# The opening of an attention-and-MoE kernel: a third load through SyncE, casts on ScalarE and GpSimd, and a new list of steps

## The chip, the cores and the metric

One core of a Trainium2 chip. The metric is the device time of one execution in microseconds; of several executions the median is taken. TensorE (PE) multiplies, VectorE (DVE), ScalarE (ACT) and GpSimd (POOL) work on its operands and results, SyncE (SP) issues transfers. POOL issues transfers too. Each engine works through its own list in order.

## What is computed

```python
# q, k, v: (8, 8, 576, 64) f32; w_in: (512, 2048); w_out: (2048, 512)
scores = q @ k.transpose(0, 1, 3, 2) / sqrt(64)
scores = where((rel >= 0) & (rel < 64), scores, -1e9)   # rel = row - column
attn = softmax(scores) @ v                              # windowed, causal
x = attn.transpose(0, 2, 1, 3).reshape(4608, 512)
h = x @ w_in
out = (h * cos(h)) @ w_out
```

## The kernel before

The 4608 tokens are worked through in nine tiles of 512 rows. For each tile PE forms h from x and w_in, ACT takes a sine of h (shifted by half of pi), DVE multiplies the two into a gate, and PE multiplies that by w_out. The attention of the next batch is woven into this by a planner that gives each piece a due time. That holds from the second tile on. Up to the end of the first tile the order is written out by hand: the string FIRST (line 45) is split into steps, and the loop at line 661 runs them one after the other. Each step appends its instructions to the lists of the engines that it uses. An engine therefore meets its instructions in the order of the string, and a wait at the head of its list holds up all that stands behind.

A step has a letter code, then numbers, then at times an engine (a is ACT, d is DVE, p is POOL, s a transfer by SP). Heads go in pairs 0 to 3. A digit that follows a score step is a PSUM bank of five.

- Lq0.p and Lk0.p load q and k of batch 0, pair p; Lq1 and Lk1 those of batch 1. Pair 0 of batch 0 is loaded as f32 by SP into a tile called rows (load_plain, line 154) and cast to bf16 by the step cq or ck (cast_plain, line 159). All the others are loaded by POOL with the cast in the transfer (load_heads, line 147). Lv, Lwi and Lwo load v, and w_in and w_out in quarters, all through POOL.
- tq, tk (batch 0) and Tq, Tk (batch 1) transpose a pair on PE, in 18 products of 64 by 64 (line 202). pq, pk, Pq, Pk copy the result from PSUM to SBUF. Their PSUM tiles come from a pool of three.
- s.p.g (line 295) forms the scores of a group of four blocks of 64 rows: two products that lay the mask into the bank (line 306), then eight of q with k (line 313). Group 0 of a pair is the first half of the tile's rows, group 1 the second. m is the maximum on DVE (line 323), e four exponentials on ACT (line 340), i the reciprocal of the sums on DVE (line 350), n the product of both (line 357, on POOL or DVE), w the transposition of the weights on PE (line 373), c its copy.
- z and y copy halves of v to the other half of the partitions. v.a.g multiplies the weights by v for half of the heads, x.a.g copies that to xT. When x.0.0 and x.1.0 are there, h for the first 256 rows can begin.
- h.g.f (line 424) forms two blocks of h for half g of the rows, S its sine (ACT), g its gate (DVE). tb and tb2 load ACT's tables for the sine and for the exponential. o.q.m (line 443) is a quarter of the second product for 128 rows, four matmuls; oc copies it out.
- Gs, Gm, Ge, Gi, Gn, Gw, Gc, Gp are the same parts of the attention for groups 8 to 18: the last block of batch 0 (8), and batch 1 (9 to 18, of three or four blocks each). Here Gm adds the mask itself (line 328), a block at a time. Gw transposes on PE; Gc lets SP transpose by a transfer. V and X close the next tile's x.

A transfer of POOL's waits until the one eight places ahead of it in POOL's list has landed.

Of the kernel before, what the change touches and what calls it, by code (L numbers as in the profile page):

```python
# [10 lines left out]
def _safe_warn(msg, *a, **kw):  # L11
# [3 lines left out]
F32 = mybir.dt.float32  # L15
# [14 lines left out]
RC = 9  # L30
# [5 lines left out]
DIRECT = (0, 7, 8)  # L36
OUTS = 3
FILL = (6, 12)
TURNED = {4: 2, 5: 2, 6: 2, 7: 6}
FAST = (7, 8)  # L40
PRODUCTS = ("P1", "P2", "P6", "P5", "P7", "P3", "P4")
# [1 line left out]


FIRST = (
# [18 lines left out]
)  # L64


# [1 line left out]
def kernel(  # L68
# [9 lines left out]
    nc = tc.nc  # L78
    B, H, S, D = q.shape
    assert (B, H, S, D) == (8, 8, 576, 64)  # L80
    scale = 1.0 / math.sqrt(D)
    d_model = H * D
    d_ff = moe_w_in.shape[1]
    n_ff = d_ff // 128
    MT = 512
# [6 lines left out]
    att = ctx.enter_context(tc.tile_pool(name="att", bufs=3))  # L92
    moe = ctx.enter_context(tc.tile_pool(name="moe", bufs=2))
# [16 lines left out]
    st = {}  # L110
# [11 lines left out]
    def copy(engine, out, in_):  # L122
        {"a": nc.scalar.copy, "p": nc.gpsimd.tensor_copy}.get(engine, nc.vector.tensor_copy)(out, in_)  # L123
# [20 lines left out]
    def rows_tile(name):  # L144
        return ld.tile([128, NC * H * D], BF16, tag=name, name=name)

    def load_heads(name, b, p0=0, n=PAIRS):
        if (name, b) not in st:
            st[name, b] = rows_tile(name)[:, 0:PAIRS * RC * D].rearrange("p (a x) -> p a x", a=PAIRS)
        src = {"q": q, "k": k}[name][b, 2 * p0:2 * p0 + 2 * n]  # L150
        nc.gpsimd.dma_start(out=st[name, b][:, p0:p0 + n],
                            in_=src.rearrange("(a h) (p c) d -> (h p) a (c d)", h=2, c=RC))

    def load_plain(name):
        rows = moe.tile([128, 2, d_model], F32, tag="out", name="rows", bufs=OUTS).rearrange("p a f -> p (a f)")[:, 0:RC * D]
        st["rows", name] = rows
        nc.sync.dma_start(out=rows, in_={"q": q, "k": k}[name][0, 0:2].rearrange("h (p c) d -> (h p) (c d)", c=RC))

    def cast_plain(name, engine):
        if (name, 0) not in st:  # L160
            st[name, 0] = rows_tile(name)[:, 0:PAIRS * RC * D].rearrange("p (a x) -> p a x", a=PAIRS)
        copy(engine, st[name, 0][:, 0], st.pop(("rows", name)))

    def load_chunk(name, b, c):
        if (name, b) not in st:
# [29 lines left out]
    def transposed(name, b, p):  # L195
# [7 lines left out]
        else:  # L203
            for c in range(TURNED.get(b, 0) if name == "q" else 0, NC):
                nc.tensor.transpose(t_ps[:, NP * c:NP * c + NP], of[:, c, 128 * p:128 * p + 128], ident[:NP, :NP])  # L205
# [9 lines left out]
    def put_q(b, p, engine=None):  # L215
        if b > 1:
            lo = TURNED.get(b, 0) * NP
            copy(engine, qsets[b % 2][:, p, lo:], st.pop(("tq", b, p))[:, lo:])
# [38 lines left out]
    for b in range(2, B):  # L257
        alone = NU // 2 if b == 3 else NU - 1
        steps = [(0, 2), (2, 4)], [(alone,)] + [(5, 7), (7, 9)] if b == 3 else [(4, 6), (6, 8), (alone,)]
# [35 lines left out]
    def g_scores(n, which):  # L295
        s_ps = bank(BANKS[which], "s_ps")
        units = groups[n]
        if n == FILL[1]:
            nc.tensor.matmul(out=s_ps, lhsT=ident, rhs=mask16[:, 0:4].rearrange("p u c -> p (u c)"), start=True, stop=True,
# [66 lines left out]
    def g_trans(n):  # L366
        w, u = st.pop(("w", n)), len(groups[n])
        if n in direct:
            st["tw", n] = t_ps = ps_t.tile([128, GF, 128], BF16, tag="t", name="tw_ps")
            for i in range(GF if n == FILL[0] else 0):  # L370
                nc.tensor.transpose(t_ps[:, i], ident, ident)
# [189 lines left out]
    def at(time, fn, *args):  # L561
        plan.append((time, len(plan), fn, args))
# [26 lines left out]
    for b in range(2, B):  # L589
        t0 = T * (b - 1)  # L590
        for c in range(TURNED.get(b, 0)):
            at(t0 - T + (24.3 if b == 4 else 23.4 if c < 2 else 26.4) + 0.01 * c, turn_q, b, c)
        for p in range(PAIRS if TURNED.get(b) != NC else 0):
            t_q = t0 + (2 if b == 2 else 1) + (3.3 if b == 2 else 3.5) * p
# [8 lines left out]
        for c in range(5):  # L603
            at(t0 + (8 if TURNED.get(b) == NC else 0.5) + c, load_v, b, c)
        for half_ in range(2):
# [16 lines left out]
    for n in range(16):  # L622
        i, f = divmod(n, 4)
# [12 lines left out]
    def spread_first(lo, hi):  # L636
        return lambda i, engine: spread_v(0, i, engine, lo, hi)

    steps = {"Lq0": lambda p: load_heads("q", 0, p, 1) if p else load_plain("q"),
             "Lk0": lambda p: load_heads("k", 0, p, 1) if p else load_plain("k"),  # L640
             "cq": lambda engine: cast_plain("q", engine), "ck": lambda engine: cast_plain("k", engine),
             "Lq1": lambda p: load_heads("q", 1, p, 1), "Lk1": lambda p: load_heads("k", 1, p, 1),
             "Lv0": lambda c: load_v(0, c), "Lv1": lambda c: load_v(1, c), "Lq2": lambda c: load_chunk("q", 2, c), "Lk2": lambda c: load_chunk("k", 2, c),
             "Lwi": lambda i: load_w_in(i * d_ff // W_PARTS, (i + 1) * d_ff // W_PARTS),
# [22 lines left out]
    for mt in range(1, n_mt):  # L667
# [5 lines left out]
        for ff in range(n_ff):  # L673
# [8 lines left out]
            e = ff % 2  # L682
# [54 lines left out]
```

## Time and profile before

| | us |
|---|---|
| median of 3 runs | 304.21 (302.83 to 304.63) |
| the profiled execution, its own time | 303.25 |
| its span, from first to last instruction | 301.5 |
| PE busy in the span | 291.7 (97%) |
| DVE, ACT, POOL busy | 233.9, 232.1, 209.1 |

The profiled execution lies 0.96 us under the median, and 1.8 us of its time lie around the span. PE's busy time is counted from modelled ends of overlapping matmuls; where it matters, the distance from one start to the next is the better measure. Idle time of an engine other than PE costs nothing by itself.

### The profile page before, as it was taken

To read this page: it belongs to the slowest core of one execution; us is meant where nothing else is said; L and a number is where in the kernel's file an instruction comes from. 1 tells how busy PE (TensorE), PEld (TensorE's weight loads), DVE (VectorE), ACT (ScalarE), POOL (GpSimd) and SP (SyncE) were. 2 spreads that over 40 slices of the span, in tenths; PEclk is the share of its full clock that TensorE was granted. 3 is DMA by queue.
4 is the path that set the end of the run, shared out by engine and by line. 5 is a ranking of instruction groups with operands and counts; after the bars stand their busy time and mean duration, and the time that the engine had idled before them with its cause. 6 is when DMAs were issued, how large, how long until landed. Compare 5 with 4: busy or idle time off the path is not lost.

```text
span 301.5 us, 8520 instructions
## 1 busy us (share of the span) xinstructions
PE 291.7 (97%) x2936; PEld 163.8 (54%) x2936; DVE 233.9 (78%) x915; ACT 232.1 (77%) x781; POOL 209.1 (69%) x238
## 2 busy tenths in 40 slices
PE   3989999999999999999999999999999999999996
PEld 2768854644455445444454445445544454785485
DVE  3798887898887886788678865887588658985794
ACT  5899699877987699769986998699978997304610
POOL 8899568996999689986998799878995860000000
PEclk9999999999999999999999999999999999999999
DMA  7999999999999994999999999999699944003013
GB/s 144 176 205 194 197 188 143 96 139 175 222 116 99 234 143 94 100 149 199 181 106 150 186 159 121 128 196 176 120 97 133 203 88 157 0 3 141 1 35 107
DMA packets 158732, 41.47 MB, mean 138 GB/s; under 512 B 146976, under 2 KB 154336, under 8 KB 158688
## 3 DMA queue, kind: packets, MB, share of 16 engines
q0 software_dynamic: 100192, 18.06, 84.0%
q1 hardware_dynamic: 58352, 22.79, 40.8%
q8 instruction: 23, 0.38, 0.5%
q14 instruction: 21, 0.17, 0.2%
q10 hardware_dynamic: 144, 0.07, 0.1%
HBM read 36.70 MB, written 9.44 MB: 153 GB/s over the span
## 4 chain that ended last, share of the span: by engine, by line
PE 80%; DMA 10%; ACT 6%; POOL 1%; issue 1%; DVE 0%; POOLq 0%; SPq 0%
PE h_ps L460 37%; PE out_ps L697 23%; PE out_ps L547 8%; DMA w_out<-in_moe_w_out_dram 6%; ACT e L340 5%; PE out_ps L443 3%; PE o_ps L392 3%; PE s_ps L291 2%; DMA wT<-w 2%; DMA k<-in_k_dram 2%; PE tq_ps L205 1%; PE s_ps L313 1%; POOL w L357 1%; PE s_ps L306 0%; ACT kT L123 0%
## 5 line engine op out<-in xcount | busy, mean ns | idle before, releaser
L460 PE MATMUL h_ps<-xT,w_in 128*128 128x512 bf16 x512 | 115.1, 379 | 0.2
L686 DVE TENSOR_TENSOR gT<-h_ps,sin 128x512 bf16<-128x512 f32 x128 | 85.2, 688 | 25.8 <-ACT sin L683 25.2
L683 ACT ACTIVATE sin<-h_ps 128x512 f32<-128x512 f32 x128 | 73.8, 598 | 37.3 <-PE h_ps L460 37.0
L340 ACT ACTIVATE e<-s,negm 128x128 f32<-128x128 f32 (+1 forms) x256 | 97.1, 381 | 2.0 <-DVE negm L328 1.0
L697 PE MATMUL out_ps<-w_out,gT 128*128 128x512 bf16 x384 | 85.3, 379 | 0.0
L357 POOL TENSOR_TENSOR w<-e,rden 128x512 bf16<-128x512 f32 (+1 forms) x68 | 69.1, 1034 | 17.0 <-DVE rden L350 12.6
L460 PEld LDWEIGHTS <-w_in 128*128 128x128 bf16 x512 | 48.9, 98 | 54.4
L697 PEld LDWEIGHTS <-gT 128*128 128x128 bf16 x384 | 36.5, 98 | 43.1
L328 DVE CUSTOM_DVE_ANT_0 s<-s_ps,mask 128x128 f32<-128x128 f32 (+1 forms) x256 | 56.0, 277 | 2.0 <-PE s_ps L313 1.7
L340 ACT ACTIVATION_READ_ACCUMULATOR e<-s,negm 128x1 f32 x256 | 48.0, 188 | 0.0
L168 POOL DMA_DIRECT2D q<-in_q_dram x36 | 28.6, 794 | 13.5 <-DMA v<-in_v_dram 5.3
L174 POOL DMA_DIRECT2D v<-in_v_dram x40 | 34.2, 869 | 1.1 <-DMA q<-in_q_dram 1.1
L168 POOL DMA_DIRECT2D k<-in_k_dram x36 | 28.5, 792 | 1.3 <-DVE gT L686 0.6
L350 DVE RECIPROCAL rden<-den 128x4 f32<-128x4 f32 (+1 forms) x73 | 12.2, 167 | 18.8 <-ACT e L340 18.5
L123 POOL COPY v<-v 64x1536 bf16<-64x1536 bf16 (+3 forms) x16 | 22.9, 1433 | 0.4
L328 DVE DVE_READ_ACCUMULATOR2_ANT negm<- 128x1 f32 x256 | 21.3, 83 | 0.0
L123 DVE CAST xT<-o_ps 128x512 bf16<-128x512 f32 x24 | 15.6, 680 | 4.9 <-PE o_ps L392 4.7
L443 PE MATMUL out_ps<-w_out,gT 128*128 128x512 bf16 x64 | 14.8, 379 | 0.2 <-DMA w_out<-in_moe_w_out_dram 0.2
L424 PE MATMUL h_ps<-xT,w_in 128*128 128x256 bf16 x128 | 14.7, 273 | 0.0
L547 PEld LDWEIGHTS <-sums 128*128 128x128 bf16 x136 | 12.2, 98 | 2.0 <-DVE sums L492 0.4
L424 PEld LDWEIGHTS <-w_in 128*128 128x128 bf16 x128 | 12.3, 98 | 1.4
L123 ACT CAST xT<-o_ps 128x512 bf16<-128x512 f32 x12 | 7.1, 612 | 6.4 <-PE o_ps L392 6.4
(85 smaller groups left out, 312.4 us busy)
## 6 DMA issues: line engine op xcount, KB each, us to landing
out_dram<-out_sb SPq DMA_DIRECT2D x16, 512.0 KB, 7.7
v<-in_v_dram POOLq DMA_DIRECT2D x32, 128.0 KB, 6.0
q<-in_q_dram POOLq DMA_DIRECT2D x36, 96.0 KB, 8.6
k<-in_k_dram POOLq DMA_DIRECT2D x36, 96.0 KB, 9.0
w_in<-in_moe_w_in_dram POOLq DMA_DIRECT2D x4, 512.0 KB, 9.0
w_out<-in_moe_w_out_dram POOLq DMA_DIRECT2D x4, 512.0 KB, 11.3
q<-in_q_dram POOLq DMA_DIRECT2D x7, 144.0 KB, 6.3
k<-in_k_dram POOLq DMA_DIRECT2D x7, 144.0 KB, 6.2
```

The costliest lines, as they stand in the source:

```text
L123: {"a": nc.scalar.copy, "p": nc.gpsimd.tensor_copy}.get(engine, nc.vector.tensor_copy)(out, in_)
L168: nc.gpsimd.dma_start(out=st[name, b][:, c].rearrange("p (h d) -> p h d", h=H), in_=src.rearrange("h p d -> p h d"))
L174: nc.gpsimd.dma_start(out=vt.rearrange("p (h d) -> p h d", h=H), in_=v[b, :, c * 128:c * 128 + n, :].rearrange("h p d -> p h d"))
L328: nc.vector.tensor_tensor_reduce(out=s[:, u, c], in0=s_ps[:, u, c], in1=mask[:, 2 - j % 2 if j else 0, c], scale=-scale if b else -1.0, sc ...
L340: nc.scalar.activation(e[:, u, c], s[:, u, c], AF.Exp, bias=negm[:, u:u + 1], scale=1.0 if n < n_first else -1.0, accum_out=den[:, u:u + 1])
L357: (nc.gpsimd if engine == "p" else nc.vector).tensor_tensor(out=w[:, 0:u], in0=e[:, 0:u], op=ALU.mult, in1=rden[:, 0:u].unsqueeze(2).to_br ...
L424: nc.tensor.matmul(out=h_ps[:, half * e:half * e + half], lhsT=w_in_sb[:, ks, ff * 128:ff * 128 + 128], rhs=st["xT", 0][:, ks, half * g:ha ...
L460: nc.tensor.matmul(out=st["h", ff], lhsT=w_in_sb[:, ks, ff * 128:ff * 128 + 128], rhs=st["xT", mt][:, ks], start=start, stop=stop)
L547: nc.tensor.matmul(out=to[n_] if split else to[:, e], lhsT=lhs[name][f // 2][:, f % 2, 128 * e:128 * e + 128], rhs=rhs[name][:, f, lo:hi], ...
L683: nc.scalar.activation(sin, h_ps, AF.Sin, bias=math.pi / 2.0)
L686: nc.vector.tensor_tensor(out=gt[:, e], in0=h_ps, in1=sin, op=ALU.mult)
L697: nc.tensor.matmul(out=o_ps[e], lhsT=gT[ff // 2][:, ff % 2, ms * 128:ms * 128 + 128], rhs=w_out_sb[:, ff], start=ff == 0, stop=ff == n_ff - 1)
```

## The change

A table PLAIN says how many pairs of batch 0 are loaded as f32 by SP: two of q, one of k. So Lq0.1 moves from POOL's queue to SP's, and cast_plain gets the pair as an argument. In the new list ACT casts both pairs of q (cq.0.a, cq.1.a) and POOL the pair of k (ck.0.p); before, DVE cast q and ACT cast k. The string FIRST is new from the first step to the last. It holds the same steps, with these differences: one load more by SP, one cast more, and the three copies of v that SP made by transfers (zB.0.s, zB.1.s, zC.s) are done by DVE and POOL. The engines of many copies differ too.

```diff
+PLAIN = {"q": 2, "k": 1}
...
-    "io Lq0.0 Lk0.0 mk cq.d mc ck.a tq.0 Lq0.1 pq.0.d Lk0.1 tk.0 pk.0.a s.0.0.0 Lq0.2 tq.1 tk.1 m.0.0 pq.1.a s.0.1.1 "
-    "Lk0.2 tq.2 pk.1.d s.1.0.2 Lq0.3 Lk0.3 tk.2 s.1.1.3 e.0.0 tq.3 m.0.1 Lq1.0 Lk1.0 Lq1.1 pq.2.d pk.2.d Lk1.1 tk.3 "
...
+    "Lq0.0 io Lk0.0 mk Lk0.1 Lq0.1 mc cq.0.a Lq0.2 Lk0.2 Lk0.3 tq.0 ck.0.p tk.1 tk.0 cq.1.a pq.0.d pk.0.d s.0.0.4 "
+    "tq.1 s.0.1.1 pk.1.a pq.1.a Lq0.3 Lk1.1 tq.2 m.0.0 s.1.0.2 tk.2 e.0.0 tk.3 m.0.1 pq.2.d pk.2.d m.1.0 i.0.0 "
+    "pk.3.a tq.3 Lk1.0 Lv0.1 Lq1.1 Lq1.0 pq.3.d Lwi.0 Lv0.0 e.0.1 s.2.0.0 Tk.1 e.1.0 s.1.1.1 s.3.0.4 s.2.1.2 "
...
-    def load_plain(name):
-        rows = moe.tile([128, 2, d_model], F32, tag="out", name="rows", bufs=OUTS).rearrange("p a f -> p (a f)")[:, 0:RC * D]
...
+    def load_plain(name, p):
+        if (name, p) == ("k", 1):
+            rows = att.tile([128, 2, MT], F32, tag="xT", name="rows", bufs=2).rearrange("p a f -> p (a f)")[:, 0:RC * D]
+        else:
+            rows = moe.tile([128, 2, d_model], F32, tag="out", name="rows", bufs=OUTS).rearrange("p a f -> p (a f)")[:, 0:RC * D]
...
+    def load_first(name, p):
+        if p < PLAIN[name]:
+            load_plain(name, p)
+        else:
+            load_heads(name, 0, p, 1)
...
+    steps = {"Lq0": lambda p: load_first("q", p), "Lk0": lambda p: load_first("k", p),
+             "cq": lambda p, engine: cast_plain("q", p, engine), "ck": lambda p, engine: cast_plain("k", p, engine),
```

Three places show what the lists of the engines became. The first is ACT, from the masks' casts to the second half of the exponentials: the cast of k or q, copies of transposed pairs (kT, qT0) out of PSUM, and groups of four exponentials (e). Before:

```order
L141 CAST mask16_83<-mask_82 128x128
L123 CAST k_108<-rows_96 128x576
L123 COPY kT_151<-tk_ps_132 128x576
L224 ACTIVATE qT0_75<-tq_ps_165 128x576
L340 ACTIVATE e_281,den_282<-s_ps_153,negm_203 128x128 x4
L340 ACTIVATE e_373,den_374<-s_ps_206,negm_306 128x128 x4
L224 ACTIVATE qT0_75<-tq_ps_287 128x576
L340 ACTIVATE e_382,den_383<-s_ps_238,negm_335 128x128 x4
```

And with the change:

```order
L143 CAST mask16_83<-mask_82 128x128
L125 CAST q_110<-rows_92 128x576
L125 CAST q_110<-rows_105 128x576
L125 COPY kT_175<-tk_ps_135 128x576
L230 ACTIVATE qT0_75<-tq_ps_188 128x576
L346 ACTIVATE e_274,den_275<-s_ps_177,negm_242 128x128 x4
L125 COPY kT_175<-tk_ps_280 128x576
L346 ACTIVATE e_335,den_336<-s_ps_207,negm_299 128x128 x4
```

The copy of a fourth pair now stands ahead of the second group of exponentials instead of behind it, and it is a copy of k; the two casts of q stand ahead of all.

The second place is POOL, from its first load to its first products of exponentials and reciprocals (w). Before:

```order
L151 DMA q<-in_q_dram 128x576
L151 DMA k<-in_k_dram 128x576
...
L174 DMA v_77<-in_v_dram 128x8x64 x4
L190 DMA w_in<-in_moe_w_in_dram 128x4x512 x3
L357 TENSOR_TENSOR w<-e,rden 128x512 x7
L190 DMA w_in<-in_moe_w_in_dram 128x4x512
```

With the change, where the first row is pair 1 of k (Lk0.1) and the CAST is ck.0.p:

```order
L153 DMA k<-in_k_dram 128x576
L153 DMA q<-in_q_dram 128x576
L153 DMA k<-in_k_dram 128x576 x2
L125 CAST k<-rows 128x576
...
L196 DMA w_in<-in_moe_w_in_dram 128x4x512
L180 DMA v_77<-in_v_dram 128x8x64 x2
L363 TENSOR_TENSOR w<-e,rden 128x512
L125 COPY v_77<-v_77 64x512
L196 DMA w_in<-in_moe_w_in_dram 128x4x512
L180 DMA v_77<-in_v_dram 128x8x64
L363 TENSOR_TENSOR w<-e,rden 128x512 x2
L196 DMA w_in<-in_moe_w_in_dram 128x4x512
```

The second and the third quarter of w_in moved behind products that wait for exponentials, and pair 1 of k is now the first load of this queue. On PE the transposition of that pair (tk_ps_135, the step tk.1) follows directly on tq.0 and stands ahead of tk.0 and of the first scores; before, the order was tq.0, tk.0, the first scores, tq.1, tk.1.

The third place is DVE around the last gates (gT), where the attention of batch 1 begins. Before, there stand the reciprocal of group 10 (rden_1092), the maximum of group 14 (s_1095), the last gate (gT_932) and the reciprocal of group 9 (rden_1108):

```order
L123 COPY kT_455<-tk_ps_1047 128x576
L350 RECIPROCAL rden_1092<-den_983 128x3
L328 ISA s_1095,negm_1094<-s_ps_1066,mask_82 128x128
...
L436 TENSOR_TENSOR gT_932<-h_ps_941,sin_955 128x2x256
L348 MEMSET e_1026 128x64
L350 RECIPROCAL rden_1108<-den_1027 128x4
```

With the change, the reciprocals of groups 11 and 12 (rden_1084, rden_1092) and the maxima of groups 13 and 14 (s_1087, s_1110):

```order
L442 TENSOR_TENSOR gT_942<-h_ps_964,sin_996 128x2x256
L354 MEMSET e_1044 128x64
L356 RECIPROCAL rden_1084<-den_1045 128x4
L334 ISA s_1087,negm_1086<-s_ps_1072,mask_82 128x64
...
L356 RECIPROCAL rden_1092<-den_1059 128x3
L334 ISA s_1110,negm_1109<-s_ps_1094,mask_82 128x128
...
L363 TENSOR_TENSOR w_1125<-e_1058,rden_1092 128x384
```

The maximum of group 14 (s_1110) now stands behind the reciprocal of group 12, which needs the tenth exponential after the table's load; on PE the scores of group 15 (Gs.15.3) need the bank that this maximum reads.

More of the change, by code (lines that the diff above doesn't have):

```diff
@@ L152, in load_heads, with cast_plain @@
                             in_=src.rearrange("(a h) (p c) d -> (h p) a (c d)", h=2, c=RC))
-    def load_plain(name):
-        rows = moe.tile([128, 2, d_model], F32, tag="out", name="rows", bufs=OUTS).rearrange("p a f -> p (a f)")[:, 0:RC * D]
-        st["rows", name] = rows
-        nc.sync.dma_start(out=rows, in_={"q": q, "k": k}[name][0, 0:2].rearrange("h (p c) d -> (h p) (c d)", c=RC))
-    def cast_plain(name, engine):
+    def load_plain(name, p):
[3 more added lines that the diff above has]
+            rows = moe.tile([128, 2, d_model], F32, tag="out", name="rows", bufs=OUTS).rearrange("p a f -> p (a f)")[:, 0:RC * D]
+        st["rows", name, p] = rows
+        src = {"q": q, "k": k}[name][0, 2 * p:2 * p + 2]
+        nc.sync.dma_start(out=rows, in_=src.rearrange("h (p c) d -> (h p) (c d)", c=RC))
+    def cast_plain(name, p, engine):
         if (name, 0) not in st:
             st[name, 0] = rows_tile(name)[:, 0:PAIRS * RC * D].rearrange("p (a x) -> p a x", a=PAIRS)
-        copy(engine, st[name, 0][:, 0], st.pop(("rows", name)))
+        copy(engine, st[name, 0][:, p], st.pop(("rows", name, p)))
     def load_chunk(name, b, c):
@@ L637, in spread_first @@
         return lambda i, engine: spread_v(0, i, engine, lo, hi)
-    steps = {"Lq0": lambda p: load_heads("q", 0, p, 1) if p else load_plain("q"),
-             "Lk0": lambda p: load_heads("k", 0, p, 1) if p else load_plain("k"),
-             "cq": lambda engine: cast_plain("q", engine), "ck": lambda engine: cast_plain("k", engine),
+    def load_first(name, p):
[5 more added lines that the diff above has]
+             "cq": lambda p, engine: cast_plain("q", p, engine), "ck": lambda p, engine: cast_plain("k", p, engine),
              "Lq1": lambda p: load_heads("q", 1, p, 1), "Lk1": lambda p: load_heads("k", 1, p, 1),
```

32 rows, old and new, of the table FIRST are left out of this document.

## Prediction

> **What bounds the kernel now.** I read the busy times of four stretches first, then the list in order of time of PE, then the chain that ended last, then ACT, DVE and the transfers. The four stretches (duration, then busy time of PE, of its weight loads, of DVE, ACT and POOL):
>
> ```profile
> 0.00:21.90 21.90, 15.62 (x385) 12.41 (x386) 15.21 (x44) 16.83 (x70) 18.68 (x32) 1.00 1.24 172
> 21.90:56.90 35.00, 34.81 (x435) 24.01 (x433) 29.12 (x118) 30.15 (x107) 27.47 (x34) 1.00 1.42 170
> 56.90:280.00 223.10, 222.72 (x1966) 113.67 (x1965) 173.78 (x721) 179.71 (x598) 162.91 (x174) 1.00 1.34 138
> ```
>
> From 21.9 us on PE idles 0.19 us up to 56.9 us and 0.38 us in the 223 us behind. So whatever delays PE in the opening is not caught up later, and only the first 21.9 us hold idle time that could be won. PE's own list (start, length, engine, line) shows the marks:
>
> ```profile
> 6.79 0.74 PE L202 MATMUL tq_ps<-ident,q 64*64 64x64 bf16 x18
> 7.75 0.69 PE L202 MATMUL tk_ps<-ident,k 64*64 64x64 bf16 x18 [0.23 <-DMA k<-in_k_dram]
> ...
> 21.91 1.95 PE L424 MATMUL h_ps<-xT,w_in 128*128 128x256 bf16 x16
> ...
> 37.42 0.47 PE L202 MATMUL tk_ps<-ident,k 64*64 64x64 bf16 x18
> 37.72 0.73 PE L202 MATMUL tq_ps<-ident,q 64*64 64x64 bf16 x36
> 38.39 1.90 PE L443 MATMUL out_ps<-w_out,gT 128*128 128x512 bf16 x8
> ...
> 56.88 2.75 PE L460 MATMUL h_ps<-xT,w_in 128*128 128x512 bf16 x12
> ```
>
> h of the first tile begins at 21.91, its last product ends at 37.42, the second tile's h begins at 56.88. What sets 21.91 is ACT:
>
> ```profile
> 7.57 0.65 ACT L224 ACTIVATE qT<-tq_ps 128x576 bf16<-128x576 bf16 x1 [1.15 <-PE tq_ps L202]
> 8.11 0.36 ACT L340 ACTIVATE e<-s_ps,negm 128x128 f32<-128x128 f32 x1
> ...
> 12.98 0.36 ACT L340 ACTIVATE e<-s_ps,negm 128x128 f32<-128x128 f32 x1
> ...
> 20.90 1.22 ACT L123 CAST xT<-o_ps 128x512 bf16<-128x512 f32 x2
> ...
> 39.54 0.39 ACT L340 ACTIVATE e<-s,negm 128x128 f32<-128x128 f32 x1
> ```
>
> The first exponential starts at 8.11 (e.0.0), the third group (e.1.0) at 12.98, and from there ACT runs without a gap to the two copies to xT at 20.90, behind which h starts. Two groups lie before 12.98, five behind it. So I ask of the new list when e.0.0 and e.0.1 start, and where PE stalls after h.
>
> **Loads at the front.** Two of the first issues, then their times to landing:
>
> ```profile
> 1.20 0.42 SPq L157 DMA_DIRECT2D rows<-in_k_dram  x1
> ...
> 1.75 0.74 POOL L151 DMA_DIRECT2D q<-in_q_dram  x1
> ```
>
> ```profile
> rows<-in_k_dram SPq DMA_DIRECT2D x1, 288.0 KB, 3.1
> ```
>
> ```profile
> q<-in_q_dram POOLq DMA_DIRECT2D x1, 144.0 KB, 4.6
> ```
>
> k's pair 0 lands at 1.20 + 3.1 = 4.3; POOL's first load at 1.75 + 4.6 = 6.35. In the new list that first load is pair 1 of k, in the same place. While it moves, SP's third load (288 KB) moves too. If the two share nothing, k.1 lands at 6.35. If it pays for all of a plain load, it comes later by what such a load costs: SP's second was down 3.1 us after its issue, with two loads in flight and part of that for the issue, so about 0.9 us, 7.2. I take the middle, 6.8, since either part is near. The Trainium skill, DMA: Bandwidth & Descriptors, section Issuing engines are not separate DMA queues, says that all queues run on the same 16 engines and interleave. By it k.1 would land at 7.2 and the sum below would be 0.4 more; the trace of before does not show the two queues at once long enough to tell.
>
> The casts: DVE's of before, and POOL's list with the issues of w_in and its first products:
>
> ```profile
> 3.64 0.46 DVE L123 CAST q<-rows 128x576 bf16<-128x576 f32 x1 [0.56 <-DMA rows<-in_q_dram]
> ```
>
> ```profile
> 12.29 2.27 POOL L190 DMA_DIRECT2D w_in<-in_moe_w_in_dram  x3
> 15.24 6.13 POOL L357 TENSOR_TENSOR w<-e,rden 128x512 bf16<-128x512 f32 x6 [0.68 <-DVE rden L350]
> ```
>
> The cast of q's pair 0 goes from DVE to ACT, behind the masks' casts; that of q's pair 1 follows. Both lie before ACT's first need (k's pair 1 transposed) and cost nothing; were they later, ACT's start would go with them, at 0.65 us each if they last as long as its copy of q (7.57). POOL's cast of k is not in the trace: between DVE's 0.46 and the 6.13 / 6 = 1.0 of a POOL product with two operands, so done between 4.8 and 5.3. It hides behind k.1's landing, since PE turns pair 1 first; without that it would hold up tk.0.
>
> **The step that is moved ahead.** PE meets tq.0, tk.1, tk.0. The transposition of pair 1 waits for POOL's load, and tk.0 with the first scores is queued behind it. From the chain that ended last (start, length): distances in it are PE's pace there, and what a copy of kT costs ACT.
>
> ```profile
> 9.29 0.48 PE tq_ps L202 x9
> 9.78 0.43 PE s_ps L306
> 10.20 0.37 PE s_ps L313 x4
> ...
> 15.88 0.53 ACT kT L123
> ...
> 47.21 0.54 PE s_ps L313 x16
> 47.75 5.29 PE out_ps L443 x24
> ```
>
> ```profile
> 8.49 0.76 DVE L123 COPY kT<-tk_ps 128x576 bf16<-128x576 bf16 x1 [0.71 <-PE tk_ps L202]
> ```
>
> tk.1 at 6.8, tk.0 at 7.3; DVE copies it 0.74 after (7.75 to 8.49), until 8.8; scores at 8.85; tq.1 0.37 behind, 9.2; ACT's copy of q 0.78 behind (6.79 to 7.57), 9.95; e.0.0 0.54 behind (7.57 to 8.11), 10.5. That is 2.4 late. Then s.0.1 waits for that copy (10.65), and PE goes on in order: tq.2 at 11.0, s.1.0 at 11.5, tk.2 at 12.3, tk.3 at 12.8. ACT's list has the copy of tk.3 ahead of e.0.1, so ACT idles from the end of e.0.0 to 12.8 + 0.74 = 13.5, and e.0.1 starts at 14.05. Behind it stand six groups and two copies before xT. Five groups and two copies took 20.90 - 12.98 = 7.92, a group (7.92 - 1.06) / 5 = 1.37; so xT comes at 14.05 + 9.3 = 23.35, 2.45 late. **First term: +2.45** (2.0 to 2.9 by k.1's landing). x.1.0 needs two copies of weights that stand on DVE behind a maximum (L328) and behind the reciprocal of the group before the last. The page's group of these maxima (count, then busy time of all):
>
> ```profile
> L328 DVE CUSTOM_DVE_ANT_0 s<-s_ps,mask 128x128 f32<-128x128 f32 (+1 forms) x256 | 56.0, 277 | 2.0 <-PE s_ps L313 1.7
> ```
>
> That group ends 1.37 before xT could start; three blocks at 56.0 / 256 = 0.22, and two copies of up to 0.76 (kT's length) make 1.4 to 2.2 with the reciprocal: none or up to 0.8 late. **Second term: +0.3**, the nearer to none since these copies are smaller. h then starts at about 24.7.
>
> **The stretch of h.** Same work for PE, one transposition (Tq.3) drawn in from behind. I followed the five banks: each h finds its bank's gate done. Nothing is added. The copies of v that leave SP are 64-partition copies on DVE and POOL; POOL's stand ahead of k.2 and k.3 of batch 1, not needed for 10 us. Cost nothing; without that cover up to 1.0 each, like a product.
>
> **Where batch 1 begins.** Let E be the end of the last h (37.42 before). ACT's first exponential comes 2.1 later (37.42 to 39.54); each takes 0.39 or a little less, so ten of them and a copy of kT (0.53) end at E + 6.5. DVE takes the reciprocal of group 12 there and only then the maximum of group 14, three blocks. At 0.22 a block that is over at E + 7.4, with 0.2 for the reciprocal. PE meanwhile does three transpositions (0.97, from 37.42 to 38.39), five quarters of the second product (0.88 each: 5.29 for six), and groups 13, 14 and 8 (about 0.28 each by 0.54 for two): 0.97 + 4.4 + 0.84 = E + 6.2. Group 15's scores want the bank of group 14 and wait 1.2. The next such place, group 18's scores, waits for DVE's copy of an output block from the same bank, by the same count up to 0.45. **Third term: +1.5** (0 to 1.7; the smaller of both in part).
>
> Then the remaining products and V, X. The longest other chain (group 16: exponentials, a product on POOL, a copy) comes out level with PE, and so does DVE's copy of v for batch 1 (y.1), which would be late next. No term; if it is one, a product's 1.0 at most.
>
> Sum: 2.45 + 0.3 + 1.5 = 4.25 us on the profiled execution's own 303.25, so 307.5. The median of the runs is 304.21, 0.96 higher: **308.5 us**.
>
> **Rivals.**
> 1. The front is late, but nothing more. For it: the third term is a race of two lists, each counted to a few tenths. Then +2.2 to +2.75 on 304.21: 306.4 to 307.0.
> 2. w_in comes late. The new list puts two of its quarters behind POOL's products; before, three were issued ahead of them (12.29):
>
> ```profile
> w_in<-in_moe_w_in_dram POOLq DMA_DIRECT2D x2, 512.0 KB, 11.4
> ```
>
> The third quarter stands behind the product of the third group, whose exponentials end at 14.05 + 3 x 1.37 = 18.2; with 6.13 / 6 = 1.0 for the product and the issues between, POOL reaches it at about 20. h.0.5 needs it near 28.4, four products of h behind 24.7. Up to 8.4 us to landing it is hidden. With the 11.4 us of the two quarters issued into a full queue before, it lands at 31.4: a stall of 3.0, 311.5.
> 3. Not slower: transfers, not ACT, set the pace of the opening. For it: the share of the transfer engines in the first two rows is 1.24 and 1.42, never idle. The change takes SP's three copies of v (320 KB, about 1 us at the pace of a plain load) out of the stream and has three loads begin early; the most that can be won is PE's idle time in the first row, 21.9 - 15.6 = 6.3, less the 4.1 before the first cast is done: 2.2. So 302.0 to 303.2. It decides when h starts no later than 21.9. Against it: PE waited only 0.19 us in the next 35, and ACT had no gap ahead of xT.
> 4. A rule gives a time of its own: a DVE copy from f32 in SBUF holds up POOL's writing of transfers. Without the cast that leaves DVE k.1 would land up to 0.46 earlier, the sum is 3.8 and the time 308.0. The Trainium skill, SBUF — State Buffer, says so in its box on the DVE blocks DMA trap, for copies in a two-port mode; no row of before shows POOL's queue held by it.
>
> **How the numbers follow.** The forecast 0.50, rival 4 0.08, rival 1 0.19, rival 2 0.10, rival 3 0.13. One per cent, 3.0 us, is about what a measurement can tell from no change here: the bounds are 301.2 and 307.25. Of the forecast and rival 4, 0.06 lies under 307.25. Slower by over 1%: 0.52 + 0.10 = 0.62. Within: 0.06 + 0.19 + 0.07 = 0.32. Faster: 0.06 of rival 3, since modelled ends may hide idle time of PE. The range 304.5 to 311.0 holds the forecast and rivals 1 and 4 and leaves out rival 3 and half of rival 2, 0.18; the forecast's own is 306.5 to 310.
>
> **What would show it.** In the changed profile: tk.1 waiting on PE for a transfer of k up to about 6.8 with nothing done behind tq.0; e.0.0 near 10.5; a gap on ACT of over 1 us before a copy of kT, then e.0.1 near 14; the first product of L430 near 24.7; scores of L319 waiting over 1 us for DVE some 6 us after the last h; the second tile's h near 61. The prediction is wrong if k.1 lands before 5.3, if h starts before 23, or if PE has no wait between the last h and the second tile.

## The result, and the profile after

The changed kernel takes 306.36 us (median of 6 runs, 306.19 to 306.79) against 303.81 us for the kernel before (6 runs, 302.83 to 304.63): a ratio of 1.0096, with a 95% interval of 1.0073 to 1.0119. It is 2.55 us slower; the point lies just under the 1% that the prediction took as the bound, and the interval holds both sides of it. Forecast were 308.5 us, with a range of 304.5 to 311.0. Direction and places held; the size was too large (4.25 us on the profiled execution, where 3.1 came), and 306.36 lies just below the 306.5 to 310 that the prediction gave its own path.

The profiled execution took 306.36 us too, with a span of 304.5 us, so 3.1 us more than the profiled execution before (303.25, span 301.5).

First the same three stretches as before, cut where h of the first tile and where h of the second begins (duration, then busy time of PE, its weight loads, DVE, ACT, POOL):

```profile
0.00:24.05 24.05, 14.81 (x386) 11.67 (x386) 16.22 (x50) 17.36 (x70) 18.91 (x33) 1.00 1.22 178
24.05:60.04 35.99, 34.77 (x435) 23.91 (x432) 29.81 (x119) 30.76 (x109) 22.93 (x29) 1.00 1.27 149
60.04:283.00 222.96, 222.72 (x1969) 113.61 (x1966) 173.92 (x718) 179.97 (x599) 162.12 (x173) 1.00 1.32 137
```

The opening grew from 21.91 to 24.05 us, the stretch behind it from 34.97 (56.88 - 21.91) to 35.99. In the rest PE idles 0.24 us: nothing is caught up there, nothing more is lost. So 2.14 us come from the front and 1.02 from the second stretch.

PE's list in order of time, at the marks of the prediction (start, length, engine, line, operation; in brackets the idle time ahead and what ended it):

```profile
6.91 1.17 PE L208 MATMUL tk_ps<-ident,k 64*64 64x64 bf16 x36 [1.41 <-DMA k<-in_k_dram]
...
10.17 0.69 PE L319 MATMUL s_ps<-kT,qT 64*64 64x128 bf16 x8
10.59 0.74 PE L208 MATMUL tq_ps<-ident,q 64*64 64x64 bf16 x18
...
11.87 0.84 PE L208 MATMUL tk_ps<-ident,k 64*64 64x64 bf16 x36
12.52 0.48 PE L208 MATMUL tq_ps<-ident,q 64*64 64x64 bf16 x18
...
24.05 2.85 PE L430 MATMUL h_ps<-xT,w_in 128*128 128x256 bf16 x24
...
39.75 0.47 PE L208 MATMUL tk_ps<-ident,k 64*64 64x64 bf16 x18
...
47.36 0.55 PE L319 MATMUL s_ps<-kT,qT 64*64 64x64 bf16 x14 [1.22 <-DVE negm L334]
...
50.55 0.80 PE L319 MATMUL s_ps<-kT,qT 64*64 64x128 bf16 x16
...
58.90 1.20 PE L398 MATMUL o_ps<-wT,v 128*64 128x64 bf16 x64
60.04 2.79 PE L466 MATMUL h_ps<-xT,w_in 128*128 128x512 bf16 x12
```

The transposition of k's pair 1 waits for its transfer until 6.91, with tk.0 behind it (36 products in one row); tq.1 follows at 9.26. The wait of 1.22 us for DVE's maximum stands where it was forecast; the short one at group 18's scores shows only as 0.80 us for 16 products (50.55). The 58.90 is V. ACT's list over the same time, and first, from the kernel before, the start of its second group:

```profile
10.07 0.37 ACT L340 ACTIVATE e<-s_ps,negm 128x128 f32<-128x128 f32 x1 [0.45 <-DVE negm L323]
```

```profile
10.58 0.36 ACT L346 ACTIVATE e<-s_ps,negm 128x128 f32<-128x128 f32 x1
...
12.75 0.64 ACT L125 COPY kT<-tk_ps 128x576 bf16<-128x576 bf16 x1 [0.67 <-PE tk_ps L208]
13.29 0.37 ACT L346 ACTIVATE e<-s_ps,negm 128x128 f32<-128x128 f32 x1
...
22.65 0.67 ACT L125 CAST xT<-o_ps 128x512 bf16<-128x512 f32 x1
23.70 0.58 ACT L125 CAST xT<-o_ps 128x512 bf16<-128x512 f32 x1 [0.37 <-PE o_ps L416]
```

The first exponential starts at 10.58 instead of 8.11, the second group at 13.29 instead of 10.07, behind the copy of pair 3 and an idle time of 0.67 (over 1 us was named as the sign). The two copies to xT no longer follow each other: 0.37 us lie between.

### The profile page after: what moved, and what is told of

Same layout as the page of the kernel before. It is cut to its first block, busy times and chain, and to the rows that moved or that the text cites. A ratio compares the mean times of both kernels' runs of the same rounds, so it can differ in the third digit from the quotient of the medians.

```text
span 304.5 us, 8506 instructions
## 1 busy us (share of the span) xinstructions
PE 290.7 (95%) x2936; PEld 162.8 (53%) x2936; DVE 235.7 (77%) x919; ACT 233.4 (77%) x785; POOL 204.0 (67%) x233
## 4 chain that ended last, share of the span: by engine, by line
PE 90%; DVE 3%; ACT 3%; DMA 2%; issue 1%; POOL 0%; POOLq 0%
PE h_ps L466 37%; PE out_ps L708 28%; PE out_ps L553 8%; PE h_ps L430 4%; PE out_ps L449 3%; PE s_ps L297 3%; PE o_ps L398 3%; ACT e L346 2%; DMA k<-in_k_dram 2%; PE tq_ps L211 1%; PE s_ps L319 1%; PE tw_ps L379 1%; DVE s L334 1%; DVE negm L329 1%; PE tk_ps L208 1%
## 5 line engine op out<-in xcount | busy, mean ns | idle before, releaser
L363 POOL TENSOR_TENSOR w<-e,rden 128x512 bf16<-128x512 f32 (+1 forms) x62 | 63.5, 1039 | 31.0 <-DVE rden L356 24.8
```

The lines of the kernel that those rows point to most:

```text
L363: (nc.gpsimd if engine == "p" else nc.vector).tensor_tensor(out=w[:, 0:u], in0=e[:, 0:u], op=ALU.mult, in1=rden[:, 0:u].unsqueeze(2).to_br ...
```

## The experiments

Each run stands beside the kernel before on its own chip (medians 303.82 for e1 to e4, 303.89 for e5 to e8, 303.33 for e9 and e10, 303.38 for e11 and e12). Two kinds of numbers are read: the median with its ratio to the kernel before, and the places in one profiled execution. The second are finer where a kernel's own landings and the pace of PE are taken into account (see e8). One time of one execution tells less: from the start of the second tile's h to the end of the execution, the fourteen profiled executions take between 246.2 and 247.5 us, in no order of their edits.

| run | median us | ratio to before (95%) |
|---|---|---|
| changed kernel | 306.36 | 1.0096 (1.0073 to 1.0119) |
| e1 tk.1 behind the first scores | 305.32 | 1.0053 (1.0036 to 1.0069) |
| e2 copy of pair 3 later | 306.82 | 1.0106 (1.0079 to 1.0133) |
| e3 maximum of group 14 first | 306.24 | 1.0080 (1.0056 to 1.0104) |
| e4 q's pair 1 by POOL | 306.14 | 1.0072 (1.0052 to 1.0093) |
| e5 e2 and maximum of group 12 later | 306.50 | 1.0076 (1.0051 to 1.0102) |
| e6 all four moves | 304.15 | 1.0014 (0.9996 to 1.0032) |
| e7 loads and casts alone, old order | 304.53 | 1.0020 (0.9998 to 1.0043) |
| e8 changed kernel again | 306.41 | 1.0086 (1.0062 to 1.0109) |
| e9 e6 and three more moves | 306.05 | 1.0087 (1.0055 to 1.0118) |
| e10 e6 without the one of group 14 | 304.46 | 1.0035 (1.0017 to 1.0053) |
| e11 kernel before, copy of q's pair 3 later | 303.41 | 1.0006 (0.9978 to 1.0035) |
| e12 e7 with tk.1 ahead of tk.0 | 305.25 | 1.0058 (1.0037 to 1.0078) |

**e1: tk.1 behind the first scores.**

```diff
-    "... tq.0 ck.0.p tk.1 tk.0 cq.1.a pq.0.d pk.0.d s.0.0.4 "
-    "tq.1 s.0.1.1 ...
+    "... tq.0 ck.0.p tk.0 cq.1.a pq.0.d pk.0.d s.0.0.4 "
+    "tk.1 tq.1 s.0.1.1 ...
```

> The changed kernel with one step moved: the transposition of k's pair 1 (tk.1) stands behind the first scores instead of ahead of tk.0. Theory (the order on PE costs the front): tk.0 starts at about 5.3 when GpSimd's cast is done instead of 7.4, the first exponential at about 9.3 instead of 10.58, the fourth pair's copy of k at about 11.6 instead of 12.75, h of the first tile at 22.8 instead of 24.05; the time is 1.2 us below the changed kernel, 305.1. Rival (the landings of POOL's loads or the stream of transfers set the pace): h starts at 24.0 all the same, 306.3. Rival (the third load through SP is what delays k): tk.1 still starts at 6.9 or later and what is gained is under 0.4 us.

Measured 305.32, 1.04 below the changed kernel. PE's list of that run, with two rows from much later:

```profile
5.31 0.67 PE L208 MATMUL tk_ps<-ident,k 64*64 64x64 bf16 x18
...
22.22 2.85 PE L430 MATMUL h_ps<-xT,w_in 128*128 128x256 bf16 x24
...
58.21 2.79 PE L466 MATMUL h_ps<-xT,w_in 128*128 128x512 bf16 x11
...
152.53 0.19 PE L398 MATMUL o_ps<-wT,v 128*64 128x64 bf16 x1 [0.42 <-DMA wT<-w]
153.23 0.98 PE L398 MATMUL o_ps<-wT,v 128*64 128x64 bf16 x51 [0.51 <-DMA wT<-w]
```

tk.0 starts at 5.31 as expected, h 1.83 and the second tile's h 1.83 earlier than in the changed kernel. The time follows only in part: in this execution PE waits 0.93 us for two transfers of weights at 152.5, which the changed kernel's profile does not show; the kernel before and most of the other runs have such waits too, of 0.2 to 0.4 us. The order on PE costs the front; with the same loads in the same places, neither their landings nor the stream of transfers set its pace.

**e2: the copy of pair 3 behind the second group.**

```diff
-    "pk.3.a tq.3 Lk1.0 ... e.0.1 s.2.0.0 Tk.1 e.1.0 ...
+    "tq.3 Lk1.0 ... e.0.1 s.2.0.0 Tk.1 pk.3.a e.1.0 ...
```

> The changed kernel with one step moved: ACT's copy of k's pair 3 (pk.3.a) stands behind the second group of exponentials instead of ahead of it. Theory: the idle 0.67 us of ACT ahead of that copy goes, the second group starts at about 12.1 instead of 13.29, the third at about 14.0 instead of 14.7, h at 23.4 instead of 24.05; 305.7. Rival (ACT does not set the start of h): h at 24.0, 306.3.

Measured 306.82: no gain. ACT's list of that run:

```profile
12.22 0.39 ACT L346 ACTIVATE e<-s_ps,negm 128x128 f32<-128x128 f32 x1
...
22.64 0.58 ACT L125 CAST xT<-o_ps 128x512 bf16<-128x512 f32 x1 [0.16 <-PE o_ps L416]
...
23.98 0.59 ACT L125 CAST xT<-o_ps 128x512 bf16<-128x512 f32 x1 [0.76 <-PE o_ps L416]
```

The second group does start 1.07 earlier (12.22), and ACT then waits in front of both copies to xT, 0.16 and 0.76. So ACT does not set the start of h alone. Three rows of busy times follow, DVE third: of the kernel before from 13.00 to 21.00 us (its h begins at 21.91), then from 13.15 to 23.20 us of the changed kernel and of e2:

```profile
13.00:21.00 8.00, 6.66 (x185) 5.09 (x181) 7.64 (x26) 8.00 (x44) 7.32 (x9) 1.00 1.72 186
```

```profile
13.15:23.20 10.05, 7.48 (x195) 5.71 (x193) 9.93 (x36) 10.05 (x52) 7.95 (x10) 1.00 1.47 172
```

```profile
13.15:23.20 10.05, 7.90 (x213) 5.88 (x209) 9.95 (x36) 9.85 (x48) 7.67 (x9) 1.00 1.43 166
```

In the changed kernel DVE is as full as ACT (9.93 of 10.05); in the kernel before it had little room too (7.64 of 8.00). The new list gave it two products that POOL made before (n.0.1, n.3.0) and the maxima of groups 11 and 12 ahead of the copies of the weights that x.1.0 needs, and took a copy of v (zA.0) from it; the copy of pair 3 of q stands in place of that of k.

**e3: the maximum of group 14 ahead of the reciprocal of group 12.**

```diff
-    "... Gi.11 Gm.13 Gi.12 Gs.14.3 o.1.0 o.2.0 Gm.14 Ge.9 ...
+    "... Gi.11 Gm.13 Gs.14.3 o.1.0 o.2.0 Gm.14 Gi.12 Ge.9 ...
```

> The changed kernel with one step moved: DVE's reciprocal of group 12 stands behind the maximum of group 14 instead of ahead of it. Theory (the bank that this maximum reads holds up the scores of group 15): PE's idle 1.22 us at 47.4 goes, the second tile's h starts 1.2 us earlier than 60.04, 305.1. Rival (another chain stands right behind it: the gates, the exponentials or a copy of v for batch 1): the wait goes to another place, over 0.7 us of it is still there, and the time is 305.8 or more.

Measured 306.24, 0.1 below the changed kernel and well short of 305.1. PE's list of that run:

```profile
46.33 0.56 PE L319 MATMUL s_ps<-kT,qT 64*64 64x64 bf16 x14 [0.31 <-ACT e L346]
...
50.15 0.41 PE L319 MATMUL s_ps<-kT,qT 64*64 64x128 bf16 x8 [0.22 <-DVE out_sb L125]
...
58.11 1.59 PE L398 MATMUL o_ps<-wT,v 128*64 128x64 bf16 x64
59.63 2.76 PE L466 MATMUL h_ps<-xT,w_in 128*128 128x512 bf16 x11
```

The wait shrinks from 1.22 to 0.31, but then the exponentials end it. From the first tile's h (23.92 here) to the second's it takes 35.71 us, against 35.99: 0.28 won of 0.91. The rest is lost again: 0.25 at group 18's scores, which now wait visibly for the copy of an output block (0.22), and 0.38 at V (1.59 us for 64 products instead of 1.20), which wants a copy that DVE makes behind y.1. The rival was right: other chains stand close behind.

**e4: q's pair 1 through POOL.**

```diff
-PLAIN = {"q": 2, "k": 1}
+PLAIN = {"q": 1, "k": 1}
-    "... tk.1 tk.0 cq.1.a pq.0.d pk.0.d s.0.0.4 "
+    "... tk.1 tk.0 pq.0.d pk.0.d s.0.0.4 "
```

> The changed kernel with q's pair 1 loaded by POOL with the cast in the transfer, as before, behind k's pair 1: SP has two loads, ACT one cast of q, the order is otherwise the same. Theory as in the prediction (the third load through SP delays k's pair 1 by about half of its transfer): k.1 lands at about 6.4 instead of 6.87, all of the front is 0.4 us earlier, 305.9. Rival (the two queues do not delay one another there): k.1 at 6.9, the same 306.3. Rival (q.1 through POOL is now late): it lands at about 7.6 against 7.1 for the cast, still ahead of its turn at 9.26, so nothing.

Measured 306.14, between the two expectations. The time from issue to landing of POOL's first load (KB, us), first in the changed kernel and here (the same row in both), then in the changed kernel again (e8), then in e11, which has the loads of the kernel before:

```profile
k<-in_k_dram POOLq DMA_DIRECT2D x1, 144.0 KB, 5.1
```

```profile
k<-in_k_dram POOLq DMA_DIRECT2D x1, 144.0 KB, 5.6
```

```profile
q<-in_q_dram POOLq DMA_DIRECT2D x1, 144.0 KB, 5.5
```

With the third load through SP it took 4.6 to 5.9 in nine profiles (mean 5.4), without it 4.6, 5.1 and 5.5 (mean 5.1). A delay of some tenths by the third load, as the prediction had it, can be neither told from this scatter nor ruled out.

**e5: e2, and the maximum of group 12 behind the copies.**

```diff
-    "... w.2.0 Gm.12 c.2.0.d w.3.0 Lq1.3 v.0.0 Gs.10.3 Gs.9.2 "
-    "Lwi.3 c.3.0.d e.1.1 ...
+    "... w.2.0 c.2.0.d w.3.0 Lq1.3 v.0.0 Gs.10.3 Gs.9.2 "
+    "Lwi.3 c.3.0.d Gm.12 e.1.1 ...
```

> The changed kernel with two steps moved: ACT's copy of k's pair 3 behind the second group of exponentials (as in the run that moved it alone), and DVE's maximum of group 12 behind the copies of the weights for x.1.0 instead of ahead of them. New theory (in the changed kernel DVE, not ACT, sets the start of h: its list has no gap from 13.1 us on): with three blocks of 0.22 us out of DVE's way, x.1.0 comes 0.65 us earlier, h starts at 23.4 instead of 24.05 (a landing of k.1 at 6.9 assumed), ACT's wait ahead of x.1.0 is about 0.1 instead of 0.76; 305.7. Rival as in the prediction (ACT sets it): ACT's own list would have allowed 23.5 already, so moving the maximum adds nothing to the run before, and h starts at 24.0 or later; 306.4.

Measured 306.50, no gain in the median. In the profiled execution PE shows:

```profile
7.68 1.17 PE L208 MATMUL tk_ps<-ident,k 64*64 64x64 bf16 x36 [2.18 <-DMA k<-in_k_dram]
...
11.20 0.47 PE L208 MATMUL tq_ps<-ident,q 64*64 64x64 bf16 x18
...
23.78 2.83 PE L430 MATMUL h_ps<-xT,w_in 128*128 128x256 bf16 x24
```

And ACT, at the start of the third group and at the copies to xT:

```profile
14.61 0.44 ACT L346 ACTIVATE e<-s_ps,negm 128x128 f32<-128x128 f32 x1
...
22.84 1.16 ACT L125 CAST xT<-o_ps 128x512 bf16<-128x512 f32 x2
```

k landed late, and h starts all the same at 23.78: 16.10 us behind tk.1, against 17.14 in the changed kernel. Part of that is PE's pace (below). But the two copies to xT follow each other without a wait, where e2 waits 0.16 and 0.76, and from the third group to h it takes 9.17 us, where e2 takes 10.02 (from 14.31 to 24.33). So in these two executions the maximum on DVE did hold up x.1.0. The median does not tell a gain; what this move alone is worth stays open.

**e6: all four moves** (e1, e5 and e3 together).

> The changed kernel with all the moves together: tk.1 behind the first scores, pk.3.a behind the second group, the maximum of group 12 behind the copies of the weights, the reciprocal of group 12 behind the maximum of group 14. If the causes add up: 1.8 at the front by tk.1, 0.65 by DVE's list, 0.3 at group 15, so the second tile's h at about 57.3 against 60.04, and 303.6, the same as the kernel before. Rival (a part of what is won is lost behind, as in the run with tk.1 alone, whose h was 1.83 earlier and whose time was only 1.0 lower): 304.5 to 305.

Measured 304.15, ratio 1.0014 (0.9996 to 1.0032): level with the kernel before within 0.3%. PE's list:

```profile
22.47 2.85 PE L430 MATMUL h_ps<-xT,w_in 128*128 128x256 bf16 x24
...
38.19 0.47 PE L208 MATMUL tk_ps<-ident,k 64*64 64x64 bf16 x18
...
58.20 2.76 PE L466 MATMUL h_ps<-xT,w_in 128*128 128x512 bf16 x11
```

The second tile's h comes 1.84 earlier than in the changed kernel, not 2.7; k landed 0.8 us later in this execution (the last section has the row), though the first exponential is only 0.30 later than in e1 (9.49 against 9.19); what else separates it from the sum is not settled.

**e7: the loads and casts alone**, in the order of the kernel before.

```diff
+PLAIN = {"q": 2, "k": 1}
-    "io Lq0.0 Lk0.0 mk cq.d mc ck.a tq.0 Lq0.1 pq.0.d Lk0.1 tk.0 pk.0.a s.0.0.0 Lq0.2 tq.1 tk.1 ...
+    "io Lq0.0 Lk0.0 Lq0.1 mk mc cq.0.a Lk0.1 Lq0.2 Lk0.2 ck.0.p tq.0 pq.0.d tk.0 pk.0.a cq.1.a s.0.0.0 tq.1 tk.1 ...
```

> The kernel before, in its old order, with the loads and casts alone: q's pair 1 by SP as f32, both casts of q on ACT, the cast of k on POOL. Theory (the new order costs, not the loads and casts): tq.0 0.65 later than 4.15, the first exponential about 0.3 later than 8.11, the third group at 12.9 to 13.1 as before, h at 21.9; 303.8, no change. Rival (the loads and casts carry the loss): h at 23 or later, 305 or more. Rival (they are a gain that the order hides): 303 or less.

Measured 304.53, ratio 1.0020 (0.9998 to 1.0043): at most 0.4%. PE's list:

```profile
7.78 0.69 PE L207 MATMUL tq_ps<-ident,q 64*64 64x64 bf16 x18 [0.16 <-ACT q L124]
...
22.33 1.96 PE L429 MATMUL h_ps<-xT,w_in 128*128 128x256 bf16 x16
```

Loaded by SP and cast by ACT, q's pair 1 is ready at 7.78; through POOL it was at 6.79. h starts 0.42 later than before. The new order carries the larger part of the loss.

**e8: the changed kernel once more.**

> The changed kernel as it is, once more, beside the others on the same chip: 306.4 as before, with the start of h within 0.3 us of 24.05 as k.1 lands. If it lies under 305.9, the gains of the single moves have been overrated against it.

Measured 306.41. Its profiled execution took 307.56 and shows why single places must be read with care:

```profile
7.39 1.17 PE L208 MATMUL tk_ps<-ident,k 64*64 64x64 bf16 x36 [1.89 <-DMA k<-in_k_dram]
...
13.33 0.72 PE L208 MATMUL tq_ps<-ident,q 64*64 64x64 bf16 x18
...
24.91 2.85 PE L430 MATMUL h_ps<-xT,w_in 128*128 128x256 bf16 x24
```

k landed 0.48 later than in the first profile, and h starts 0.86 later. The other 0.38 goes with PE's pace: a transposition of 18 products still takes 0.72 at 13.33, where it took 0.48 at 12.52 in the first. My expectation of 0.3 us was too narrow.

**e9: three more moves on e6.**

```diff
-    "... n.2.0.p c.0.0.d c.1.0.d i.3.0 n.3.0.d zA.1.d ... v.0.0 Gs.10.3 Gs.9.2 "
-    "Lwi.3 c.3.0.d Gm.12 e.1.1 x.0.0.a v.1.0 m.3.1 x.1.0.a ...
+    "... n.2.0.p i.3.0 n.3.0.d c.0.0.d c.1.0.d zA.1.d ... v.0.0 "
+    "Lwi.3 c.3.0.d Gm.12 x.0.0.a v.1.0 Gs.10.3 Gs.9.2 m.3.1 x.1.0.a e.1.1 ...
```

> The kernel with all four moves, and three more at the front: the reciprocal and product of the fourth group (i.3.0, n.3.0, DVE) ahead of the copies of the weights instead of behind them, the scores of groups 10 and 9 on PE behind v.1.0 instead of ahead of it, and the exponentials of group e.1.1 on ACT behind the two copies to xT. Theory (the lists of DVE and ACT set the start of h, not the loads): both copies to xT are ready 0.8 to 1.1 us earlier than 21.26 and 22.12, h at about 21.5 instead of 22.47; the sines follow in the same order and do not hold up PE; 303.2, under the kernel before by 0.6. Rival (what is taken from the front is only put off: e.1.1 then delays the second half of x, and PE waits for it before h of that half): h at 21.5, but the last h no earlier than in the run with four moves, 304.2. Rival (w_in is late for an earlier h): PE waits for a transfer of w_in within the first eight h, 304 or more.

Measured 306.05: 1.9 worse than e6. PE's list:

```profile
21.95 1.04 PE L430 MATMUL h_ps<-xT,w_in 128*128 128x256 bf16 x8
...
26.04 1.05 PE L430 MATMUL h_ps<-xT,w_in 128*128 128x256 bf16 x8 [0.71 <-DVE negm L334]
...
38.97 0.47 PE L208 MATMUL tk_ps<-ident,k 64*64 64x64 bf16 x18
```

h starts 0.5 earlier than in e6 (0.3 of it because k landed earlier: the first exponential is at 9.20 instead of 9.49), and its last product ends 0.8 later (38.97 against 38.19): the exponentials and maxima that were put off now hold up PE inside the stretch of h. The first rival named the mechanism. That explains 0.8 us; the other 1.1 of the median stays open.

**e10: e6 without the move of group 14.** The edit is e6 with the line of e3 as it was.

> The kernel with all four moves less the one of group 14's maximum: tk.1 behind the first scores, pk.3.a and the maximum of group 12 later, as in the kernel with all moves. If the single moves add up: 0.3 above that kernel's 304.15 (PE's wait of 1.2 us for that maximum is back, of which the chains behind gave back 0.9 when it was removed alone), so 304.45, and 0.7 to 0.9 below the run with tk.1 alone (305.3). Rival (the 1.2 us count in full once the front is early): 305.2 or more, the same as with tk.1 alone.

Measured 304.46, 0.3 above e6 by the medians and 0.6 by the ratios, whose intervals overlap; by the ratios 0.5 below e1. PE's wait is back in full:

```profile
45.82 0.55 PE L319 MATMUL s_ps<-kT,qT 64*64 64x64 bf16 x14 [1.22 <-DVE negm L334]
```

The second tile's h comes 36.01 us behind the first (58.49 - 22.48) against 35.73 in e6. Twice, then, a visible wait of 1.22 us was worth 0.28.

**e11: the kernel before, with the copy of q's pair 3 behind the third group.**

```diff
-    "... e.0.1 pq.3.a i.0.0 e.1.0 Tk.0 ...
+    "... e.0.1 i.0.0 e.1.0 pq.3.a Tk.0 ...
```

> The kernel before with one step moved: ACT's copy of q's pair 3 (pq.3.a) stands behind the third group of exponentials (e.1.0) instead of ahead of it. Theory (in the kernel before ACT alone sets the start of h, DVE has room): ACT's idle 0.86 us ahead of that copy shrinks to the 0.9 us or less until the third group's maximum is there, the third group starts at about 12.45 instead of 12.98, h at 21.4 instead of 21.91; 303.3, or 0.5 us below the kernel before. Rival (DVE's or PE's list is as close there as in the changed kernel): h at 21.8 or later, no change.

Measured 303.41 against 303.38: no change. The profiled execution lies 1.67 above the median (305.08), with a landing of 5.5 us; ACT's list in it:

```profile
12.84 0.37 ACT L340 ACTIVATE e<-s_ps,negm 128x128 f32<-128x128 f32 x1 [0.98 <-DVE negm L323]
```

The idle time ahead of the copy turned into one ahead of the exponentials, which wait for DVE's maximum. The row bears the rival out: in the kernel before, too, ACT is not alone in setting the pace. The median by itself could not tell, since its interval (0.9978 to 1.0035) holds the 0.5 us of the theory.

**e12: e7 with tk.1 ahead of tk.0.**

```diff
-    "... tq.0 pq.0.d tk.0 pk.0.a cq.1.a s.0.0.0 tq.1 tk.1 m.0.0 ...
+    "... tq.0 pq.0.d tk.1 tk.0 pk.0.a cq.1.a s.0.0.0 tq.1 m.0.0 ...
```

> The kernel with the loads and casts alone (old order otherwise) with one step moved: tk.1 directly behind tq.0, ahead of tk.0 and the first scores, as in the changed kernel. Theory (this place of tk.1 is the larger part of the loss): tk.0 waits for k's pair 1 and starts at 7.4 to 8.1 instead of 5.6, the first exponential at 10.5 to 11.2 instead of 9.05, h 1.0 to 1.5 later than the 22.33 of the loads alone, 305.6 to 306.0 against 304.5. Rival (the loss needs the rest of the new order, above all the copy of pair 3 ahead of the second group): ACT catches up, h is less than 0.5 later, 305.0 or less.

Measured 305.25, ratio 1.0058 against the 1.0020 of e7: 0.38%, 1.2 us, for this place alone, near the lower end of what was expected (1.1 to 1.5 above e7) and about what e1 won back (1.0); the two intervals overlap a little. The profiled execution was the fastest of its runs (303.79); k landed early in it, after 4.6 us:

```profile
6.41 1.17 PE L207 MATMUL tk_ps<-ident,k 64*64 64x64 bf16 x36 [0.90 <-DMA k<-in_k_dram]
...
22.59 1.95 PE L429 MATMUL h_ps<-xT,w_in 128*128 128x256 bf16 x16
```

```profile
10.16 0.36 ACT L345 ACTIVATE e<-s_ps,negm 128x128 f32<-128x128 f32 x1
```

tk.0 stands behind that landing, and the first exponential is 1.11 later than in e7 (10.16 against 9.05). But the third group is only 0.27 later (13.68 against 13.41) and h 0.26 (22.59 against 22.33): in this execution ACT catches up, as the rival had it. That the later landings of other executions make up the rest of the 1.2 is argued, not shown.

## Why the prediction came out as it did

**The landing of k's pair 1: 6.8 forecast, about 6.9 measured, for a reason that is not shown.** The prediction had the third load through SP delay it. In e4 that load is gone, and k takes the same 5.1 us; with the loads of before (e11) POOL's first load took 5.5. Since landings scatter from 6.4 to 7.6, that the first profile met 6.8 is luck. The Trainium skill, DMA: Bandwidth & Descriptors, section Issuing engines are not separate DMA queues, would have it at 7.2 by the working in the prediction; landings of 6.4 to 7.6 in the runs with the third load neither bear that out nor refute it. Rival 4 is as open: without DVE's cast the first load came no earlier in the changed kernel (5.1 us against 4.6), and the scatter is wider than the 0.46 in question. Its rule is in the Trainium skill, SBUF — State Buffer, in the box on the DVE blocks DMA trap.

**The first exponential: 10.5 forecast, 10.58 measured.** The chain tk.1, tk.0, copy, scores, tq.1, copy of q, exponential came out link by link. e1 shows it by undoing it (9.19) and e12 by making it alone (10.16 against 9.05 in e7).

**The second group: 14.05 forecast, 13.29 measured. This step failed.** The prediction let s.0.1 wait for the copy of q's pair 1 until 10.65. s.0.1 is the second half of pair 0 and does not need it: PE starts it at 10.17 and goes on with tq.2 at 10.59 instead of 11.0. PE's products also became shorter before tk.3 (0.84 for the 36 from 11.87). So the first and the second term together are 2.14 instead of 2.75. The sum behind that point, 9.3 us to xT, was right (22.65 - 13.29 = 9.36), and so was the 0.3 for x.1.0 (0.37).

**"What sets 21.91 is ACT"** was incomplete, for the changed kernel and for the one before. e2 frees ACT and gains nothing: DVE's list, full from 13.15 to 23.20, ends at the same time, and with one maximum out of it (e5) ACT no longer waits for xT. In the kernel before, e11 moves ACT's gap, and ACT waits for DVE instead (0.98). The second term was the edge of that: DVE behind ACT by 0.4, not a detail.

**The stretch of h: nothing forecast.** From the start of h to its end 15.70 us (39.75 - 24.05) against 15.51, with one transposition drawn in. Right.

**The third term: 1.5 forecast, 0.83 measured** from the end of the last h to the second tile's h (20.29 us, 60.04 - 39.75, against 19.46), or 1.1 with the transposition that moved out of this stretch. The wait stands there with 1.22, but its worth is 0.28 (e3, e10). The prediction took a wait as a cost because PE stood; it had itself noted that group 16's chain and y.1 come out level with PE, and priced them at nothing. Taking the wait away (e3) shows y.1: three smaller waits take its place, 0.31 for exponentials, 0.25 at group 18's scores and 0.38 at V behind y.1. No run took these away, so how the 0.83 divides among the lists stays open; for group 16's chain no run shows anything.

**The sum.** 2.14, 0.19 and 0.83 on the profiled execution's 303.25 give 306.4, what was measured. To that the prediction added 0.96 because the median then lay above the profiled run; of the six runs it is 0.56, and the changed kernel's profiled run lies on its own median. So of the 2.1 us by which the forecast was too high, 1.1 are the terms (0.7 too much in the first and 0.7 in the third, less 0.2 in the stretch of h and 0.1 in the second) and 1.0 is this step.

**The rivals.** Rival 1, the front and nothing more, gave 306.4 to 307.0 and came nearest, though not by its mechanism: the second stretch does cost, and the number fits because rival 1 starts from the median of three runs, 0.4 above that of six. Rival 2 is refuted: no wait for w_in is seen, its quarters took a median of 6.2 us to land. Rival 3 is refuted by the start of h at 24.05 and by e1, which moved it by 1.83 with the same loads.

How the loss divides, by the runs: the loads and casts alone 0.2% (e7, not told from zero), tk.1 ahead of tk.0 0.4% (e1, e12), the copy of pair 3 with the maximum of group 12 about 0.2% (e1 against e10), the maximum of group 14 about 0.1 to 0.2% (e10 against e6). The intervals of e1, e10 and e6 overlap from each to the next, and e1 was measured on another chip, so the last two shares are estimates. No version that was run is faster than the kernel before.

## What to carry to other kernels

A step put ahead of another on an in-order engine hands its own wait on to it: ask of each swap which of the two operands lands first, and whom the earlier one feeds. A gap on the engine that sets the end is not yet a gain: look which other list ends at the same time, and count the wait only down to that; two moves that do next to nothing alone (e2, e3) can belong to a set that brings nearly all of it back (e6). And when a step is costed, look up which data it reads, by its pair and half, before it is given a wait.

## What the runs showed of the hardware

POOL's first load of 144 KB, issued within 0.01 of 1.75 in every run, took from 4.6 us (the kernel before, its row is in the prediction) to 5.9 us from issue to landing; the means with three and with two loads by SP beside it, 5.4 and 5.1, lie closer than two executions of one kernel (5.1 and 5.6). A front that hangs on it moves by as much: in e8 it came 0.48 later than in the first profile, and the first exponential did too (11.06 against 10.58). The longest, in e6:

```profile
k<-in_k_dram POOLq DMA_DIRECT2D x1, 144.0 KB, 5.9
```

The moment at which PE's products become shorter also moves: a transposition of 18 products falls from 0.74 to 0.48 by 12.52 in the changed kernel's first profile, still takes 0.72 at 13.33 in its second, and has fallen by 11.20 in e5, while the column of the granted clock reads 1.00 throughout. The Trainium skill, TensorE: Matmul & The Clock Gate, section What's actually happening, states that the array runs at half its clock until a window of about 3.4 us was busy, and that these windows run freely, not from the kernel's start. The two profiles of one kernel, at least 0.8 us apart in this, agree with that in kind; no row here shows the clock itself at half.
